# Bulk loads moved to one queue and paced, and the second transform shifted by one group, in a spectral filter fused with a gated FFN

## The chip, the cores and the metric

The kernel runs on one core of a Trainium2 chip. The metric is the device time of one execution in microseconds (us). A profile is one execution, about 2 us shorter than the timed runs of the same kernel, because its span goes from the first to the last instruction.

## The reference, cut to what matters

```python
xn  = layernorm(x)                       # x: 2048 x 640, bf16
s   = irfft2(rfft2(xn) * (A_w_r + 1j * A_w_i))          # filter: 2048 x 321
g   = silu((gelu(xn @ w_gate) * (xn @ w_up)) @ w_down)  # FFN, 1536 wide
out = x + s * g
```

The rows are cut into 16 slabs of 128. The FFN needs the transposed xn and the weights. The filter needs a Fourier transform over all slabs, so it cannot begin before every slab is normalised and folded.

## The kernel before: the parts that matter

TensorE (PE) does nearly all of the work as matmuls. The FFN is a list of 64 items: four groups of twelve gate/up tiles and four downs. All else is hooked behind an item. A scheduler then orders the instructions of each engine, so the order in the source is a priority, not the order on the chip.

Six names of tiles serve as milestones in the profiles: `pg` and `pu` are the gate and up matmuls, `ph` a down, `pa` the fold of a slab, `pzt` the first matmul of the spectral stage (its copy is `ztail`, the name that the prediction uses), and `pv` the first of the inverse.

```python
for q in range(4):                                   # weights: issued by ACT
    nc.scalar.dma_start(out=Wg[:, :, cs], in_=gv[:, :, cs])
    nc.scalar.dma_start(out=Wu[:, :, cs], in_=uv[:, :, cs])
nc.gpsimd.dma_start(out=LANE, in_=tabs["lane"])      # row numbers for the gathers
nc.scalar.dma_start(out=Wd, in_=...)                 # then seven tables, also by ACT
...
def norm(n1):
    if n1 % 3 == 0:   # statistics on DVE
        ...           # bn_stats x2, bn_aggr; POOL adds the epsilon to the variance
    else:             # statistics on ACT, with two accumulating activations
        ...           # POOL turns the sums into mean and variance
    nc.gpsimd.tensor_tensor(out=rstd, in0=rstd, in1=mh, op=ALU.pow)
    nc.vector.tensor_scalar(out=xn, in0=x, scalar1=mean, scalar2=rstd, ...)
    # slabs 0-3: PE transposes and ACT copies; later slabs: a DMA transpose from SP
def fold(n1):
    ...               # DVE: four adds give xf; PE: pa = F1T^T xf; ACT: A = pa
    nc.sync.dma_start(out=D2[:, n1, :], in_=A)       # scratch in HBM
def regroup():        # BU <- D2, needs all sixteen stores
    ...
def gather(G):        # filter weights of group G: four indirect DMAs by POOL
    nc.gpsimd.memset(W[:, :, :, L:LP], 0.0)
    for pm in range(2):
        for ri, wsrc in enumerate((A_w_r, A_w_i)):
            nc.gpsimd.indirect_dma_start(out=W[:, pm, ri, 0:L], in_=wsrc, ...)
def spectral_a(G):    # PE z, ACT Z, PE pe, ACT E, DVE V
def spectral_b(G):    # DVE: M, N = W * V, Y, R;  PE: pi = BD R;  ACT, DVE: IU;  store
...
for i in range(12):
    after[i].append((norm, 4 + i))                   # and the folds
    if i in (5, 7, 9, 11):
        after[i].append((gather, (i - 5) // 2))
after[11].append((regroup,))
for G in range(8):
    i = 14 + 2 * G
    after[i].append((spectral_a, G))
    after[i + 1].append((spectral_b, G))
    if G < 4:
        after[i + 1].append((gather, G + 4))
after[29].append((reload,))
```

So POOL has two jobs: tiny steps (rstd) that every slab waits for, and indirect loads (gathers).

## Time and profile before

The time before is 262.58 us (median of 3 runs, 262.43 to 263.23). In the profile (span 259.9 us):

| milestone | us |
|---|---|
| first gate matmul | 36.36 |
| first down | 68.29 |
| first matmul of the spectral stage | 78.07 |
| first matmul of the inverse | 173.75 |
| end | 259.9 |

The first lines are of the page of the kernel before: busy tenths of PE and of the DMA engines in 40 slices of 6.5 us, and what the DMAs moved.

```profile
PE   0010079999999999999999877779999999999881
DMA  7999993657283032141210110174431012110110
GB/s 216 386 338 327 358 371 83 175 142 196 94 291 115 20 84 63 45 100 44 57 55 0 51 51 3 51 270 186 138 118 53 23 61 70 50 50 3 50 50 25
```

PE is almost idle in the first five slices, busy after them, and dips in slices 23 to 27, which is the end of the spectral stage. The DMA engines are full just where PE is idle.

The timeline of ACT, kernel before: start, duration, engine (ACTq is its DMA issuing), line, operation, and in brackets the idle time before it.

```profile
8.83 4.12 ACTq L208 DMA_DIRECT2D Wu<-in_B_w_up_dram  x1
12.99 2.57 ACTq L207 DMA_DIRECT2D Wg<-in_B_w_gate_dram  x1
...
19.75 4.83 ACTq L212 DMA_DIRECT2D T_77<-tab_t  x1
...
27.39 0.68 ACTq L212 DMA_DIRECT2D IT<-tab_it  x1
28.11 0.69 ACT L245 COPY xnT<-pt 128x640 bf16<-128x640 bf16 x1 [25.37 <-issue]
28.70 0.74 ACT L233 ACTIVATE junk<-X 128x640 bf16<-128x640 bf16 x1
```

An issue normally takes 0.4 to 0.7 us here. Three of them take 2.6 to 4.8 us. ACT does no arithmetic from 2.7 to 28.1 us, because its stream is full of issues, and its first statistics come at 28.70.

What POOL does in that time, timeline of POOL, kernel before:

```profile
7.52 1.01 POOL L282 DMA_INDIRECT W<-in_A_w_r_dram,LANE  x1 [5.33 <-DMA LANE<-tab_lane]
...
27.31 0.95 POOL L282 DMA_INDIRECT W<-in_A_w_i_dram,LANE  x1 [0.30 <-issue]
29.62 0.25 POOL L236 TENSOR_SCALAR mean<-nm 128x1 f32<-128x1 f32 x1 [1.37 <-ACT junk L233]
```

The sixteen gathers of the first four groups run from 7.5 to 28.3 us, about 1.25 us each.

The waits of PE from 0 to 78 us, kernel before (waiter, what it waited for: us in total, times, longest):

```profile
PE pt L244 <- DVE xn L240: 32.6, 3, 17.9
PE pa L260 <- ACT xnT L245: 0.5, 1, 0.5
PE pa L260 <- DVE xf L258: 0.4, 2, 0.2
```

And from 70 to 180 us:

```profile
PE pi L356 <- DVE R L345: 5.8, 7, 1.9
PE pv L375 <- DMA BU<-D_93: 1.4, 1, 1.4
PE pe L317 <- DVE G_1542 L428: 1.2, 1, 1.2
PE ph L423 <- ACT E L324: 0.6, 2, 0.4
```

Once started, PE hardly waits in the fold stage.

### The profile page before, as it was taken

The page shows a single profiled execution, that of the slowest core. Times are in us where ns is not written, and L with a number is a line of the kernel's source. Part 1 is how long each engine was busy: PE and PEld are TensorE (multiplying, and loading weights), DVE is VectorE, ACT ScalarE, POOL GpSimd, SP SyncE. Part 2 cuts the span into 40 slices and gives each one's busy share as a digit, 9 for nine tenths or more (in the row PEclk, how much of TensorE's full clock was granted, in tenths as well). Part 3 has the DMA queues.
Part 4 walks back from the last instruction along what each step waited for, and adds up shares of the span by engine and source line. Part 5 has one row for each costly group of instructions (what it writes and reads, how often), then busy time and mean ns, then how long its engine had stood idle before and what let it go on. Part 6 is the DMA issues. An engine that isn't in the chain of part 4 may idle for free. (4 is left out here: it accounts for less than half of the span.)

```text
span 259.9 us, 3724 instructions
## 1 busy us (share of the span) xinstructions
PE 208.8 (80%) x1348; PEld 118.2 (45%) x1348; DVE 144.5 (56%) x337; ACT 117.5 (45%) x192; POOL 50.2 (19%) x87
## 2 busy tenths in 40 slices
PE   0010079999999999999999877779999999999881
PEld 0000034444575554454454454545567654456660
DVE  1430177998223957756658435448954555653562
ACT  2000689995427264464553514246542445343431
POOL 1777444662000426236000000000000000000000
PEclk9999999999999999999999999999999999999998
DMA  7999993657283032141210110174431012110110
GB/s 216 386 338 327 358 371 83 175 142 196 94 291 115 20 84 63 45 100 44 57 55 0 51 51 3 51 270 186 138 118 53 23 61 70 50 50 3 50 50 25
DMA packets 30385, 31.61 MB, mean 122 GB/s; under 512 B 10384, under 2 KB 28576, under 8 KB 30240
## 3 DMA queue, kind: packets, MB, share of 16 engines
q1 hardware_dynamic: 20992, 20.42, 24.6%
q10 hardware_dynamic: 7808, 8.33, 9.7%
q0 software_dynamic: 1568, 2.64, 4.0%
q8 instruction: 10, 0.16, 0.3%
q14 instruction: 7, 0.06, 0.1%
HBM read 21.53 MB, written 7.88 MB: 113 GB/s over the span
## 5 line engine op out<-in xcount | busy, mean ns | idle before, releaser
L409 PE MATMUL pg<-xnT,Wg 128*128 128x512 bf16 x240 | 63.5, 384 | 0.0
L411 PE MATMUL pu<-xnT,Wu 128*128 128x512 bf16 x240 | 62.2, 380 | 0.0
L423 PE MATMUL ph<-Wd,u 128*128 128x320 bf16 x384 | 53.9, 299 | 1.0 <-ACT E L324 0.6
L423 PEld LDWEIGHTS <-u 128*128 128x128 bf16 x384 | 37.4, 98 | 16.1 <-issue 1.6
L415 DVE TENSOR_TENSOR u<-pu,ge 128x512 bf16<-128x512 f32 x48 | 32.9, 686 | 20.9 <-PE pu L411 17.1
L413 ACT ACTIVATE ge<-pg 128x512 bf16<-128x512 f32 x48 | 28.9, 602 | 18.6 <-PE pg L409 16.1
L411 PEld LDWEIGHTS <-Wu 128*128 128x128 bf16 x240 | 23.2, 98 | 24.5 <-issue 0.8
L409 PEld LDWEIGHTS <-Wg 128*128 128x128 bf16 x240 | 22.3, 99 | 22.7 <-issue 1.1
L426 ACT ACTIVATE th<-ph 128x640 f32<-128x640 f32 x16 | 11.3, 704 | 42.6 <-PE ph L423 42.6
L244 PE MATMUL pt<-ident,xn 128*128 128x128 bf16 x20 | 2.7, 310 | 32.6 <-DVE xn L240 32.6
L282 POOL DMA_INDIRECT W<-in_A_w_r_dram,LANE x16 | 15.4, 965 | 11.0 <-DMA LANE<-tab_lane 5.3
L244 PEld LDWEIGHTS <-xn 128*128 128x128 bf16 x20 | 1.8, 135 | 33.2 <-DVE xn L240 33.2
L282 POOL DMA_INDIRECT W<-in_A_w_i_dram,LANE x16 | 15.4, 965 | 4.8 <-issue 4.8
L356 PE MATMUL pi<-R,BD 128*128 128x322 bf16 x64 | 10.8, 301 | 6.4 <-DVE R L345 5.8
L324 ACT CAST E<-pe 128x644 bf16<-128x644 f32 x16 | 13.1, 888 | 4.6 <-PE pe L322 4.6
L240 DVE TENSOR_SCALAR xn<-X,mean,rstd 128x640 bf16<-128x640 bf16 x10 | 4.4, 443 | 18.4 <-POOL rstd L238 18.2
L359 ACT CAST IU<-pi 128x644 bf16<-128x644 f32 x8 | 5.6, 696 | 19.8 <-PE pi L356 19.8
L245 ACT COPY xnT<-pt 128x640 bf16<-128x640 bf16 x4 | 2.6, 687 | 25.8 <-issue 25.4
L382 ACT CAST Vt<-pv 128x640 bf16<-128x640 f32 x16 | 11.1, 692 | 7.0 <-PE pv L379 7.0
L263 ACT CAST A<-pa 128x640 bf16<-128x640 f32 x16 | 10.9, 697 | 4.3 <-DMA D_92<-A 2.6
L327 DVE TENSOR_TENSOR V<-E 128x644 bf16<-128x644 bf16 x8 | 4.0, 495 | 13.4 <-ACT E L324 13.3
L356 PEld LDWEIGHTS <-BD 128*128 128x128 bf16 x64 | 5.6, 97 | 12.6 <-DVE R L345 9.1
(175 smaller groups left out, 272.4 us busy)
## 6 DMA issues: line engine op xcount, KB each, us to landing
D_93<-IU SPq DMA_DIRECT2D x8, 322.0 KB, 2.9
BU<-D_93 SPq DMA_DIRECT2D x4, 644.0 KB, 6.6
xr<-in_A_x_dram SPq DMA_DIRECT2D x16, 160.0 KB, 2.4
D_92<-A SPq DMA_DIRECT2D x16, 160.0 KB, 2.0
BU<-D_92 SPq DMA_DIRECT2D x4, 640.0 KB, 7.5
out_dram<-res SPq DMA_DIRECT2D x16, 160.0 KB, 1.8
Wg<-in_B_w_gate_dram ACTq DMA_DIRECT2D x4, 480.0 KB, 10.9
Wu<-in_B_w_up_dram ACTq DMA_DIRECT2D x4, 480.0 KB, 10.2
```

The lines of the kernel that those rows point to most:

```text
L263: nc.scalar.copy(out=A, in_=flat(pa)[:, 0:D])
L282: nc.gpsimd.indirect_dma_start(out=W[:, pm, ri, 0:L], out_offset=None, in_=wsrc, in_offset=bass.IndirectOffsetOnAxis(ap=LANE[:, 2 * G + pm ...
L324: nc.scalar.copy(out=E[:, ri].rearrange("p r (i q) -> p r q i", q=2), in_=pe[:, :, 0:LP].rearrange("p r (q i) -> p r q i", q=2))
L356: nc.tensor.matmul(pi[:, pq, 0:LP], lhsT=BD[:, G, ro, ri, :], rhs=R[:, ri, pq, :], start=(ri == 0), stop=(ri == 1))
L359: nc.scalar.copy(out=IU[:, ro], in_=pi[:, :, 0:LP])
L382: nc.scalar.copy(out=flat(Vt), in_=pvf[:, 0:D])
L409: nc.tensor.matmul(pg, lhsT=Wg[:, c, t * P:(t + 1) * P], rhs=xnT[:, c, cols], start=(c == 0), stop=(c == 4))
L411: nc.tensor.matmul(pu, lhsT=Wu[:, c, t * P:(t + 1) * P], rhs=xnT[:, c, cols], start=(c == 0), stop=(c == 4))
L413: nc.scalar.activation(out=ge, in_=pg, func=ACT.Gelu_apprx_tanh)
L415: nc.vector.tensor_tensor(out=u, in0=pu, in1=ge, op=ALU.mult)
L423: nc.tensor.matmul(ph[:, a, 0:320], lhsT=uT[grp, t][:, j * P:(j + 1) * P], rhs=Wd[:, t, 320 * a:320 * a + 320], start=(t == 0), stop=(t == ...
L426: nc.scalar.activation(out=th, in_=ph[:, :, 0:320], func=ACT.Tanh, scale=0.5)
```

## The change

The intent is twofold. The load half puts all bulk loads on SP, in the order in which they are needed, and issues the later ones between the slabs' own transposes and stores; it also moves the statistics of five slabs from ACT to DVE, and the xr loads to POOL. The spectral half emits spectral_b one group later, so that PE has a whole group of other work between E and pi.

```diff
+    ctx.enter_context(tc.manual_schedule(engines={mybir.EngineType.SP}))
-    for q in range(4):
-        nc.scalar.dma_start(out=Wg[:, :, cs], in_=gv[:, :, cs])
-        nc.scalar.dma_start(out=Wu[:, :, cs], in_=uv[:, :, cs])
+    def load_gu(q): ...   # the same two loads, on nc.sync; likewise load_x, load_d, load_tab
+    load_x(0, 1); load_x(1, 2); load_tab("id"); load_x(2, 4); load_gu(0)   # [joined]
+    load_x(4, 8); load_tab("f1"); load_gu(1); load_x(8, 12); load_x(12, 16)
@@ norm
-        if n1 % 3 == 0:
+        if n1 % 3 != 2:
@@ final
-        nc.sync.dma_start(out=xr, in_=xv[:, n1, :])
+        nc.gpsimd.dma_start(out=xr, in_=xv[:, n1, :])
@@ hooks
+    after[0].append((load_gu, 2))
+    after[1].append((load_gu, 3))
+    after[2].append((load_tab, "t2"))
+    after[3].append((load_tab, "fm", "ft"))
+    after[4].append((load_d, 0))
+    after[6].append((load_d, 1))
+    after[8].append((load_tab, "bd", "i1", "im", "it"))
-        after[i + 1].append((spectral_b, G))
+        after[i + 3].append((spectral_b, G))
-            after[i + 1].append((gather, G + 4))
+            after[i + 3].append((gather, G + 4))
-    after[29].append((reload,))
+    after[31].append((reload,))
```

Engines named in `manual_schedule` keep the order of the source; the others are still ordered by the scheduler.

More of the change, by code (lines that the diff above doesn't have):

```diff
@@ L199, with load_x, load_gu, load_d @@
     nc.scalar.activation(out=warm, in_=warm, func=ACT.Gelu_apprx_tanh)
-    for a, b in ((0, 1), (1, 2), (2, 4), (4, 8), (8, 12), (12, 16)):
+    def load_x(a, b):
         nc.sync.dma_start(out=X[:, a:b, :], in_=xv[:, a:b, :])
-        if a == 2:
-            nc.sync.dma_start(out=F1T, in_=tabs["f1"])
-            nc.sync.dma_start(out=ident, in_=tabs["id"])
-    for q in range(4):
+    def load_gu(q):
         cs = slice(q * 384, q * 384 + 384)
-        nc.scalar.dma_start(out=Wg[:, :, cs], in_=gv[:, :, cs])
-        nc.scalar.dma_start(out=Wu[:, :, cs], in_=uv[:, :, cs])
-    nc.gpsimd.dma_start(out=LANE, in_=tabs["lane"])
-    nc.scalar.dma_start(out=Wd, in_=B_w_down.rearrange("(t p) d -> p t d", p=P))
-    for t, k in ((T2, "t2"), (FM, "fm"), (FT, "ft"), (BD, "bd"), (I1T, "i1"), (IM, "im"), (IT, "it")):
-        nc.scalar.dma_start(out=flat(t), in_=tabs[k])
+        nc.sync.dma_start(out=Wg[:, :, cs], in_=gv[:, :, cs])
+        nc.sync.dma_start(out=Wu[:, :, cs], in_=uv[:, :, cs])
+    def load_d(h):
+        nc.sync.dma_start(out=Wd[:, 6 * h:6 * h + 6, :],
+                          in_=B_w_down.rearrange("(t p) d -> p t d", p=P)[:, 6 * h:6 * h + 6, :])
+    def load_tab(*ks):
+        for k in ks:
+            nc.sync.dma_start(out=flat(tiles[k]), in_=tabs[k])
+    tiles = dict(f1=F1T, id=ident, t2=T2, fm=FM, ft=FT, bd=BD, i1=I1T, im=IM, it=IT)
+    nc.gpsimd.dma_start(out=LANE, in_=tabs["lane"])
+    load_x(0, 1)
+    load_x(1, 2)
+    load_tab("id")
+    load_x(2, 4)
+    load_gu(0)
+    load_x(4, 8)
+    load_tab("f1")
+    load_gu(1)
+    load_x(8, 12)
+    load_x(12, 16)
     xn_of, y_of, G_of, W_of = {}, {}, {}, {}
```

## The prediction

> **What bounds it now.** Over the span TensorE (PE) is the bound: busy 80% (208.8 us), nearly 100% from 40 to 140 us and from 180 to 240 (stage table). Its idle time: (a) the start: the first gate matmul runs at 36.4 us; (b) 7.4 us between 140 and 174 us, the end of the spectral stage, waiting for R on DVE (1.9, 1.3, 0.6 us), and 1.4 us for the reload; (c) 7.7 us in the tail from 240.
>
> Why (a): the DMA share is 1.0 (about 350 GB/s) from 10 to 40 us, and ACT issues the weight loads. Its issues block while the queue is full: the timeline has ACT issuing from 0.75 to 28.1 us, one issue lasting 4.8 us, so the statistics of slabs 1 and 2 on ACT start only at 28.7. PE waits 18 us for one xn.
>
> **What changes.**
> 1. All bulk loads go to SP, in order of need, the last between transposes and D2 stores. The Trainium skill, "DMA: Bandwidth & Descriptors", section "Issuing engines are not separate DMA queues", says all issuers share the same 16 engines, so one queue should cost no bandwidth; the trace shows 1.0 share reached. The first matmul needs 1.6 MB, an estimated 5 us at 350 GB/s.
> 2. Statistics of five slabs (1, 4, 7, 10, 13) move from ACT (about 1.95 us a slab) to DVE (0.89+0.20 us).
> 3. xr loads move to POOL; three come first in its order.
> 4. spectral_b one group later: the built PE order has a whole group of filler between e(G+1) and pi(G), and about 8 us of gate/up between the last pi and the first inverse.
>
> **Cost on the critical path.**
> New start: the next limit is POOL, which in order runs LANE, three xr (about 1 us each), then gathers (1.25 us each) between the rstd operations. Estimate: first gather at 6 to 6.6 us, slabs 0-2 normalised at about 14.5, then three more gathers, so rstd of slab 3 at about 21 us, first gate matmul at about 23 us. Gain 13 us.
> Fold stage: DVE was about 90% occupied from 42 to 65 us. It gets seven more slabs of statistics in it (7.6 us), so I sum about 33 us of DVE for 31 us of PE: DVE-bound, 2 to 3 us given back. SP is tight too (issues: about 29 us). The first down (68.3 us before) then starts at about 57.
> Spectral end: of 7.4 us I expect 6 saved.
> Sum: 262.6 - 13 + 2.5 - 6 - about 1 for small waits = 245.
>
> **Predicted: 245 us, 8 in 10 between 238 and 252.** Faster by over 2%: 0.96; within 2%: 0.03; slower: 0.01.
>
> **What would show each step.** ACT's first statistics at about 5 us; xn of slab 3 released by POOL rstd after gathers; first gate matmul at 20 to 26 us; DVE over 90% busy in the fold stage, PE waiting there for xf or u by 2 to 4 us; the first ztail matmul at 66 to 70 us; waits of pi for R under 2 us in total; no wait of pv for the reload; same last 20 us.
>
> **What would make it wrong.** LANE landing early or late shifts the POOL chain by its whole delay. SP in program order: a transpose waiting for xn holds stores and loads behind it; stores hold A buffers, A holds fold matmuls; a late D2 store delays the regroup and PE stalls before ztail. Late weights behind slab traffic. xr on POOL landing late in the tail.

## The result

The changed kernel takes 251.62 us (median of 4 runs, 251.30 to 251.76) against 262.5 us (4 runs). The ratio is 0.9578, with a 95% interval of 0.9558 to 0.9597. All ratios here are the mean time of one kernel's fast runs over the mean of the other's in the same rounds, so they are not quite the ratio of the medians. Executions over 1.5% slower than the fastest of the same kernel are left out of the means. The outputs are right.

The time lies inside the predicted range, close to its upper end, and 6.6 us above the centre. The milestones show that the parts were far less right than the sum:

| us | before | after | difference |
|---|---|---|---|
| first gate matmul | 36.36 | 24.70 | -11.7 |
| first down | 68.29 | 67.54 | -0.8 |
| first spectral matmul | 78.07 | 77.32 | -0.8 |
| first inverse matmul | 173.75 | 157.67 | -16.1 |
| end of the span | 259.9 | 249.8 | -10.1 |

PE starts 11.7 us earlier, and 10.9 us of that are gone 40 us later. The first inverse matmul gains more than the end does, because the shift also moves FFN work from before it to behind it.

The page of the kernel after, the same lines:

```profile
PE   0032947987999999889999999899999999999981
DMA  6996599999967022313101013833111111110110
GB/s 192 348 369 181 115 219 285 249 266 327 220 172 277 0 67 82 111 61 108 53 7 49 14 42 111 364 109 106 52 55 52 52 55 52 52 52 3 52 54 26
```

PE has work in the third slice now, but it has gaps up to the tenth. The DMA engines ease off in slices 4 and 5 and are then full to about 69 us. The dip at the end of the spectral stage is gone.

The timeline of ACT, after: no issues, and the first statistics at 6.12 us instead of 28.70.

```profile
2.04 0.20 ACT L201 ACTIVATE warm<-warm 128x1 f32<-128x1 f32 x1
6.12 0.74 ACT L250 ACTIVATE junk<-X 128x640 bf16<-128x640 bf16 x1 [3.88 <-DMA X<-in_A_x_dram]
```

The timeline of POOL, after: L299 is a gather, L245 and L255 are the steps of rstd.

```profile
22.05 1.65 POOL L255 TENSOR_TENSOR rstd<-rstd,mh 128x1 f32<-128x1 f32 x3
23.84 1.20 POOL L299 DMA_INDIRECT W<-in_A_w_r_dram,LANE  x1
...
33.29 0.95 POOL L299 DMA_INDIRECT W<-in_A_w_i_dram,LANE  x1 [0.30 <-issue]
34.31 0.23 POOL L245 TENSOR_SCALAR rstd<-mva 128x1 f32<-128x1 f32 x1
34.62 0.57 POOL L255 TENSOR_TENSOR rstd<-rstd,mh 128x1 f32<-128x1 f32 x1
```

What hangs on it, timeline of DVE, after:

```profile
22.68 0.98 DVE L257 TENSOR_SCALAR xn<-X,mva,rstd 128x640 bf16<-128x640 bf16 x2 [4.80 <-POOL rstd L255]
...
35.23 0.45 DVE L257 TENSOR_SCALAR xn<-X,mva,rstd 128x640 bf16<-128x640 bf16 x1 [7.59 <-POOL rstd L245]
35.59 0.68 DVE L432 TENSOR_TENSOR u<-pu,ge 128x512 bf16<-128x512 f32 x1
```

And timeline of PE, after:

```profile
24.70 2.29 PE L426 MATMUL pg<-xnT,Wg 128*128 128x512 bf16 x5
26.79 2.34 PE L428 MATMUL pu<-xnT,Wu 128*128 128x512 bf16 x5
...
30.39 1.24 PE L428 MATMUL pu<-xnT,Wu 128*128 128x512 bf16 x5
...
36.32 2.29 PE L428 MATMUL pu<-xnT,Wu 128*128 128x512 bf16 x5 [3.34 <-DVE u L432]
...
67.54 2.74 PE L440 MATMUL ph<-Wd,u 128*128 128x320 bf16 x19
```

These three views are one chain. From 23.84 to 34.24 us POOL issues eight gathers in a row, broken once by a 0.28 us step. The rstd of a slab stands behind them. DVE meets its xn (7.59 us of waiting), and the u that DVE could have computed stands behind that xn in DVE's order; PE needs u to free a buffer in PSUM, the memory that its matmuls write, and waits 3.34 us.

Then PE pays again: five matmuls take 2.29 us at 36.32 but 1.24 us at 30.39. The Trainium skill, "TensorE: Matmul & The Clock Gate", section "Part 1: The HAM clock gate (the "warmup" mystery)", says that after an idle window of about 3.4 us PE runs at half rate until a window of about 3.4 us is busy again. The trace agrees: its record of the granted clock is 0.5 for 3.4 us here, and the mean granted clock from 30 to 40 us is 0.83.

The waits of PE from 0 to 78 us, after:

```profile
PE pt L261 <- DVE xn L257: 21.0, 2, 15.8
PE pu L428 <- DVE u L432: 3.3, 1, 3.3
PE pa L277 <- DVE xf L275: 2.7, 2, 1.4
PE pa L277 <- ACT A L280: 0.8, 1, 0.8
```

The stage from the first gate to the first down takes 42.8 us instead of 31.9. Of these 10.9 us, 6.4 are waits of PE (3.3 + 2.7 + 0.8 - 0.4). About 1.6 are the half-rate matmuls from 36.3 to 40.2 us, counting each at its time at full rate elsewhere in the trace. About 0.9 more is a longer slow phase at the very start: the first five up matmuls take 2.34 us (at 26.79) against 1.47 before (at 38.45), and the first ten gate/up matmuls with one fold take 4.61 us against 3.67. And 1.7 are no loss: the scheduler's new order puts eight more gate/up matmuls (0.216 us each) ahead of the first down. About 0.3 us are not accounted for.

In the spectral stage, waits of PE from 70 to 180 us, after:

```profile
PE pi L373 <- issue: 1.1, 2, 0.7
PE pz L322 <- DVE IU L378: 0.8, 1, 0.8
PE pv L392 <- DMA BU<-D_93: 0.6, 1, 0.6
```

No wait of pi is put down to R any more. With four of 0.2 to 0.4 us that are not shown, the waits sum to 3.6 us instead of 10.0.

### The profile page after: what moved, and what is told of

Same layout as the page of the kernel before. It is cut to its first block, busy times and chain, and to the rows that moved or that the text cites. A ratio compares the mean times of both kernels' runs of the same rounds, so it can differ in the third digit from the quotient of the medians.

```text
span 249.8 us, 3706 instructions
## 1 busy us (share of the span) xinstructions
PE 209.1 (84%) x1327; PEld 119.4 (48%) x1348; DVE 147.8 (59%) x352; ACT 110.5 (44%) x172; POOL 56.3 (23%) x98
## 5 line engine op out<-in xcount | busy, mean ns | idle before, releaser
L426 PE MATMUL pg<-xnT,Wg 128*128 128x512 bf16 x226 | 61.9, 386 | 0.7 <-issue 0.2
L450 POOL DMA_DIRECT2D xr<-in_A_x_dram x16 | 8.8, 551 | 110.9 <-DVE res L454 108.6
L299 POOL DMA_INDIRECT W<-in_A_w_r_dram,LANE x16 | 16.6, 1037 | 6.9 <-issue 3.2
L299 POOL DMA_INDIRECT W<-in_A_w_i_dram,LANE x16 | 15.7, 980 | 4.5 <-issue 4.4
L257 DVE TENSOR_SCALAR xn<-X,mva,rstd 128x640 bf16<-128x640 bf16 x11 | 5.0, 451 | 17.7 <-POOL rstd L255 10.0
L242 DVE BATCH_NORM_STATS2 stats<-X 128x6 f32<-128x320 bf16 x22 | 10.2, 485 | 8.6 <-DMA X<-in_A_x_dram 8.6
L325 ACT CAST Z<-pz 128x1024 bf16<-128x1024 f32 x8 | 8.1, 1011 | 5.2 <-PE pz L322 5.2
```

Source lines behind the costliest of these rows:

```text
L242: nc.vector.bn_stats(out=stats[:, g, :], in_=x[:, 320 * g:320 * g + 320])
L299: nc.gpsimd.indirect_dma_start(out=W[:, pm, ri, 0:L], out_offset=None, in_=wsrc, in_offset=bass.IndirectOffsetOnAxis(ap=LANE[:, 2 * G + pm ...
L426: nc.tensor.matmul(pg, lhsT=Wg[:, c, t * P:(t + 1) * P], rhs=xnT[:, c, cols], start=(c == 0), stop=(c == 4))
```

## The experiments

Twelve kernels ran. The ratios are to the kernel before, run on the same chip. Milestones are from the profiles.

| run | first gate | first down | spectral | inverse | span | ratio, 95% interval |
|---|---|---|---|---|---|---|
| before | 36.36 | 68.29 | 78.07 | 173.75 | 259.9 | 1 |
| after | 24.70 | 67.54 | 77.32 | 157.67 | 249.8 | 0.9578 [0.9558, 0.9597] |
| e1_loads_only | 24.51 | 67.30 | 77.08 | 175.55 | 261.6 | 1.0036 [0.9982, 1.0090] |
| e2_shift_only | 36.05 | 67.98 | 77.76 | 157.02 | 249.2 | 0.9634 [0.9581, 0.9686] |
| e3_pool_program_order | 14.11 | 63.02 | 72.80 | 150.44 | 242.6 | 0.9342 [0.9290, 0.9394] |
| e4_stats_on_act | 21.07 | 62.26 | 72.04 | 149.76 | 241.9 | 0.9323 [0.9260, 0.9386] |
| e5_gathers_last | 14.07 | 52.13 | 72.28 | 152.40 | 244.5 | 0.9308 [0.9254, 0.9361] |
| e6_gathers_last_stats_act | 14.42 | 64.49 | 75.13 | 153.63 | 245.8 | 0.9358 [0.9313, 0.9402] |
| e7_loads_unpaced | 14.11 | 66.21 | 77.87 | 155.42 | 247.6 | 0.9485 [0.9413, 0.9557] |
| e8_shift_gathers_last | 33.41 | 67.53 | 87.67 | 167.06 | 259.2 | 0.9991 [0.9944, 1.0038] |
| e9_old_stats_pool_order | 14.11 | 59.16 | 68.94 | 146.75 | 238.9 | 0.9168 [0.9120, 0.9216] |
| e10_no_early_gathers | 14.08 | 50.37 | 60.15 | 137.84 | 230.0 | 0.8869 [0.8815, 0.8924] |
| e11_late_tables | 20.01 | 58.93 | 68.71 | 147.86 | 240.0 | 0.9262 [0.9200, 0.9323] |
| e12_gathers_after_regroup | 14.14 | 50.56 | 60.34 | 144.09 | 236.2 | 0.9092 [0.9053, 0.9131] |

One caution for reading it. The scheduler puts 120 to 144 gate/up matmuls ahead of the first down, depending on the kernel (120 in before, e2, e8 and e11; 128 in after, e1 and e4; 136 in e3, e5, e6, e9, e10 and e12; 144 in e7), which moves that milestone and the next by up to 5.2 us without any work saved. The ratio is the measure; the milestones say where to look.

### e1: the load half alone

```diff
 (the change, but with these lines as before)
-        after[i + 3].append((spectral_b, G))
+        after[i + 1].append((spectral_b, G))
-    after[31].append((reload,))
+    after[29].append((reload,))
```

> The change without its second half: loads, statistics split and xr on POOL as in the changed kernel, but spectral_b, gather and reload at their old places. Theory A (from the two traces: the load half starts PE 11.7 us earlier but the fold stage gives nearly all of it back, so the first down matmul moves by only 0.75 us, and the gain comes from the spectral half): 260 to 262.5 us, first gate matmul at about 25 us, first down at about 67.5 us, waits of pi for R as before. Rival B (the sum of the prediction: the load half is worth about 10 us): 251 to 254 us.

Measured: 262.76 us, ratio 1.0036. The load half alone gains nothing, although PE starts 11.9 us earlier. At the first down only 1.0 us of it is left, and the waits for R have grown, as the waits of PE from 70 to 180 us of e1 show:

```profile
PE pi L373 <- DVE R L362: 8.3, 6, 5.1
```

### e2: the spectral half alone

```diff
 (the kernel before, with)
-        after[i + 1].append((spectral_b, G))
+        after[i + 3].append((spectral_b, G))
-            after[i + 1].append((gather, G + 4))
+            after[i + 3].append((gather, G + 4))
-    after[29].append((reload,))
+    after[31].append((reload,))
```

> The kernel before with only the spectral half (spectral_b and gather one group later, reload two items later); loads on two queues as before. Theory A: 252 to 254 us, that is 9 to 10 us of gain from this half alone, first gate matmul at 36.4 and first down at about 68.3 us as before, waits of pi for R near zero. Rival B (prediction): 256 to 257 us (6 us).

Measured: 252.07 us, ratio 0.9634, or 9.6 us of 262.5. So this half carries nearly the whole gain of the change. All waits of pi for R are gone, and the waits of PE from 70 to 180 us sum to 2.2 us. The product of the ratios of the two halves is 0.967; the change itself is at 0.958. The halves together may be 1% better than that product, about as much as the intervals allow, and I make nothing of it.

What remains to be explained is why 11.7 us of earlier start are worth nothing.

### e3: POOL in the order of the source

The scheduler had put gathers ahead of rstd steps. Here POOL keeps the order of the source, where the first gather comes behind item 5.

```diff
-    ctx.enter_context(tc.manual_schedule(engines={mybir.EngineType.SP}))
+    ctx.enter_context(tc.manual_schedule(engines={mybir.EngineType.SP, mybir.EngineType.Pool}))
```

> The changed kernel with the instructions of POOL, too, kept in program order: the gathers of A_w_r and A_w_i and the xr loads then stand behind the rstd operations of slabs 0 to 9, instead of 16 gathers standing among those of slabs 0 to 6. Theory P (the gathers on POOL hold back rstd, that holds back xn of slabs 3 and 6, and through DVE's order also u and PE): first gate matmul at 14 to 17 us, no wait of DVE for rstd over 2 us in the fold stage, 240 to 245 us. Rival D (DVE is overloaded by the statistics moved to it): earlier start, but DVE over 90% busy and first down not before 62 us, 246 to 249 us. Rival S (the order on SP holds D2 stores and with them A and PE): 248 to 252 us.

Measured: 244.52 us, ratio 0.9342, 2.4% better than the change. The first gate moves to 14.1 us. The gathers are still in the way later on: each batch of four stands between rstd steps. DVE waits 13.0 us for rstd from 14 to 66 us, and PE 9.0 us for xf. So theory P had the time right, but not its "no wait of DVE for rstd over 2 us": the longest is 4.0 us.

### e4: the old split of the statistics

```diff
-        if n1 % 3 != 2:
+        if n1 % 3 == 0:
```

> The changed kernel with the old split of the statistics (DVE for slabs 0, 3, 6, 9, 12, 15; ACT for the others). Theory P: the fold stage is not set by DVE's load, so 250 to 253 us, within 1% of the changed kernel. Rival D: 5.5 us less DVE work in the fold stage, so 3 to 5 us faster, 247 to 249 us.

Measured: 243.80 us, ratio 0.9323. I had put the weight on POOL and expected little of this run; that was a miss, and even rival D's 247 to 249 us was too slow. Moving five slabs of statistics to DVE costs about 2.7% (0.9578 against 0.9323). It was meant to relieve ACT, but once ACT issues no loads it has time: in the change ACT is busy only 3.2 to 5.4 us of every 10 from 0 to 60, while DVE is at 9.5 and 9.3 of 10 from 40 to 60.

### e5 and e6: gathers behind the norms

e5 is e3 with the first sixteen gathers moved behind the last norm; e6 is e5 with the old statistics.

```diff
-        if i in (5, 7, 9, 11):
-            after[i].append((gather, (i - 5) // 2))
     after[11].append((regroup,))
+    for G in range(4):
+        after[12].append((gather, G))
```

> The changed kernel with POOL in program order and the 16 gathers of the first four frequency groups emitted after the last rstd (about 20 us of POOL work, not needed before the first spectral_b). Statistics as in the changed kernel (11 slabs on DVE). Theory P (gathers on POOL between the rstd operations starve DVE and then PE; e3 showed the same stalls moved later): first gate matmul at 14 us, no wait of DVE for rstd over 2 us, first down at 49 to 53 us, 231 to 236 us. Rival D (DVE's load sets the fold stage): first down at 54 to 58 us, 236 to 240 us. Rival S (the order of SP sets it): no better than e3, 242 to 245 us.

> The run with the gathers last, with the old split of the statistics as well (DVE 6 slabs, ACT 10). Theory P alone: the same as the run before within 1.5 us. Theory P with D: another 2 to 4 us faster, 229 to 234 us. If ACT becomes the limit (20 us of statistics in the fold stage): slower than the run with the statistics on DVE.

Measured: 245.48 us for e5 (median of three fast runs; the slow fourth took 249.00; ratio 0.9308) and 246.57 us for e6 (0.9358). Both miss what I expected, e5 by 10 us, and with the gathers here the old split of the statistics brings nothing: the two intervals overlap. The rstd chain is free, and yet the time is no better than in e3. POOL now issues the gathers back to back at the end of the fold stage (38.0 to 58.4 us in e6), and there the other engines stop for long stretches. These are lines of the waits from 40 to 66 us, e6:

```profile
ACT ge L430 <- remote: 9.9, 1, 9.9
DVE u L432 <- ACT ge L430: 7.0, 1, 7.0
DVE xf L274 <- issue: 6.9, 1, 6.9
ACT A L280 <- issue: 5.7, 2, 5.4
PE pa L277 <- ACT A L280: 4.4, 1, 4.4
```

"issue" and "remote" mean that the profile shows no releaser. Around 50.6 us ACT and DVE both go on within 0.1 us of each other, after waiting on PE's semaphore, though by its records PE had done that work at 47 us. The granted clock stays at 0.5 for 17 us.

### e7: all loads up front

```diff
 (e6, with these right behind load_x(12, 16) instead of in items 0 to 8)
+    load_gu(2)
+    load_gu(3)
+    load_d(0)
+    load_d(1)
+    load_tab("t2", "fm", "ft", "bd", "i1", "im", "it")
```

> As the run with the gathers last and the old split of statistics, but all bulk loads issued at the start on SP in the same order of need, not paced between transposes and D2 stores. If the pacing matters: transposes and D2 stores wait behind about 9 MB of loads (an estimated 27 us at 350 GB/s), fold matmuls stop for A, 6 us or more slower than the paced one. If it does not: within 2 us.

Measured: 249.66 us, ratio 0.9485 against 0.9358 of e6. So giving up the pacing costs e6 about 3 us, between the two readings (6 or more, within 2). It is not a clean price of the pacing: e7 has a stall like e6's, beside gathers that run from 43.2 to 63.9 us (DVE waits 11.6 us for a u, with no visible releaser, and PE 9.8 us for an A, the copy of a fold), and what the loads add to it was not separated.

### e8: gathers last with the old loads

```diff
 (e2, with)
+    ctx.enter_context(tc.manual_schedule(engines={mybir.EngineType.Pool}))
 (and the gathers moved as in e5)
```

> The kernel before with the spectral half of the change (as e2) and with POOL in program order and the gathers after the last rstd. Theory P says that in the kernel before the gathers ran in the shadow of ACT's blocked load issues (7.5 to 28 us) and cost nothing: 251 to 253 us, as e2. If the gathers cost time there too: 245 to 249 us.

Measured: 262.34 us, ratio 0.9991, where I had expected e2's 252; neither expectation fits. With the old loads, moving the sixteen gathers out of the idle start costs all that the shift gains. They then run from 56 to 77 us, and the same long stalls as in e6 appear (DVE once 9.3 us). So the idle start is by far the cheaper place. The run does not show that the gathers are free there. The timeline of PE, e8:

```profile
33.41 2.29 PE L411 MATMUL pg<-xnT,Wg 128*128 128x512 bf16 x5
```

In e2 that first gate runs at 36.05. Without gathers in the start ACT's issues end sooner (first statistics at 25.63 us, 28.40 in e2), so at their old place the gathers cost up to 2.6 us of the start. That their transfers slow the loads down is the likely reason; it was not tested.

### e9: both repairs that helped alone

e3 and e4 together.

> The changed kernel with both repairs that helped alone: the old split of the statistics and POOL in program order. Theory F (before the regroup the DMA engines have 62 to 69 us of work in every kernel so far, so ztail cannot start before about 71 us, whatever the start): first gate near 14, ztail 71 to 73, time 241 to 244, no better than either repair alone. Theory S (the repairs remove separate waits of POOL and DVE and add): ztail 65 to 68, time 235 to 239.

Measured: 240.30 us, ratio 0.9168. The two repairs add, though not fully: the separate gains over the change are 2.4 and 2.6 points of the ratio, and together they give 4.1. The time falls between the ranges of theory F (241 to 244) and theory S (235 to 239), and so does the start of the spectral stage at 68.9 us (F: 71 to 73, S: 65 to 68). Neither theory as written is right.

### e10: no early gathers (wrong result)

```diff
 (e6, with)
     def gather(G):
+        if G < 4:
+            nc.gpsimd.memset(W, 0.0)
+            W_of[G] = W
+            return
```

> The kernel with gathers last and the old statistics, without the 16 gathers of groups 0 to 3 (their weights are zero: wrong on purpose). They move 1.3 MB of about 19.4 MB that land before ztail. Theory G (gathers running beside dense work cause the long stalls of ACT, DVE and PE at 49 to 66 us): no wait over 4 us in 40 to 66 us, first down near 56, ztail 60 to 65, time 230 to 236. Theory F (the DMA work before the regroup is the floor): ztail about 4 to 5 us earlier than the 75.1 us with gathers, so 70 to 71, time 240 to 242.

Measured: 231.91 us, ratio 0.8869; the result is wrong (relative error 0.028). Against e6 this is 4.9 points of the ratio, about 13 us. The long stalls are gone, the granted clock is 0.999, and PE is 94% busy from 10 to 60 us (46.9 us of 50). So the sixteen gathers, at the place where e6 has them, cause the stalls. That is theory G's time. As theory F was written, from the bytes, it is refuted: 1.3 MB less should have been worth 4 to 5 us ahead of the spectral stage, and 15 us came.

### e11: tables after the regroup

```diff
 (e4, with)
-    after[8].append((load_tab, "bd", "i1", "im", "it"))
     after[11].append((regroup,))
+    after[12].append((load_tab, "bd", "i1", "im", "it"))
```

> The changed kernel with the old statistics split, and the 1.4 MB of tables that only the filter and the inverse need loaded after the regroup instead of in item 8. Theory F: about 4 us less DMA work before the regroup, so ztail about 68 instead of 72, time 239 to 241. Rival (ztail waits for the compute engines, not for DMA): ztail 71 to 73, time 243 to 245.

Measured: 242.19 us, ratio 0.9262 against 0.9323 of e4, with intervals that overlap. The spectral stage starts 3.3 us earlier, as F said, but eight gate/up matmuls fewer stand ahead of it (1.7 us), so only 1.6 us are real, and the span is 1.9 us shorter. The time lies between the two expectations. Taking 1.4 MB out of the crowded stage is worth something like 2 us, half of what theory F gave for a pure DMA limit; as the intervals overlap, no gain at all is not excluded.

### e12: gathers held back until the regroup

POOL first copies one column of the regrouped slabs into a tile that nobody needs. As POOL keeps the order of the source, the gathers stand behind that copy.

```diff
 (e6, with)
+    def hold_pool():
+        nc.gpsimd.tensor_copy(out=warm, in_=hop["B"][:, 12, 0:1])
 ...
+    after[12].append((hold_pool,))
     for G in range(4):
         after[12].append((gather, G))
```

> The kernel with gathers last and the old statistics (246.6 us), with one tiny POOL copy from the regrouped slabs ahead of the 16 gathers, so that they start only when the DMA work of the fold stage is over (about 60 us) and run back to back to about 80 us, with 8 instead of 20 us or more of other DMA traffic beside them. Theory C (the gathers hurt where they meet the full DMA queues of the fold stage): ztail near 60 as without the early gathers, no wait over 4 us in 60 to 80 us, granted clock above 0.98, time 231 to 235, the best version. Theory B (16 gathers back to back stall the other engines wherever they run): ztail near 60, but stalls of 5 us or more and half clock between 60 and 80 us, time 238 to 247.

Measured: 237.94 us (6 runs, 237.01 to 239.62), ratio 0.9092: correct, and the fastest correct version, 9% below before and 5% below the change. One tiny instruction on POOL is worth 7 us against e6, by the ratios. The timeline of PE, e12:

```profile
14.14 2.29 PE L429 MATMUL pg<-xnT,Wg 128*128 128x512 bf16 x5 [0.71 <-ACT xnT L262]
...
50.56 9.94 PE L443 MATMUL ph<-Wd,u 128*128 128x320 bf16 x72
...
60.34 0.39 PE L316 MATMUL pzt<-T,BU 128*128 128x128 bf16 x4
```

Up to here it equals the kernel without early gathers. The stalls without a visible releaser do not come back, although the gathers run back to back from 66 to 87 us; that speaks against theory B's mechanism. But the run also misses the 231 to 235 us of theory C, and some of what B foretold is there: PE waits 4.5 us once, ACT 5.4 us once, the granted clock is 0.5 for 3.4 us from 76.7 us, and the time is at the lower edge of B's range. These waits have a reason that is plain in the trace. The hold waited for the last quarter of the regroup and let the gathers start at 65.2 us, not 60. Timeline of POOL, e12:

```profile
65.16 0.18 POOL L295 CAST warm<-BU 128x1 f32<-128x1 bf16 x1 [27.60 <-DMA BU<-D]
```

The first filter product then had to wait for its gathers, and the G of a down stood behind it on DVE, which PE needed. Timeline of DVE and of PE, e12:

```profile
72.79 0.83 DVE L359 TENSOR_TENSOR M<-W,V 128x1288 bf16<-128x1288 bf16 x1 [4.26 <-DMA W<-in_A_w_i_dram,LANE]
```

```profile
75.95 0.44 PE L337 MATMUL pe<-FT,ztail 128*128 128x322 bf16 x2 [4.53 <-DVE G L448]
```

In e10 that M starts at 68.18. The gathers of group 0 leave POOL at 70.91 and release M at 72.79. The Trainium skill, "Perfetto Trace Analysis", section "DMA Instruction — SWDGE (GPSIMD)", says that the recorded end of such an instruction is the end of descriptor generation, not of the data movement; the 1.9 us between the two times agree with that. A hold on the first quarter, or only three groups held back, may take these 4.5 us away; that was not run.

## Why the prediction was right or wrong, point by point

The sum missed by 7.4 us in the profile, nearly all of it in one term. That the time still fell inside the range, by 0.4 us, was luck. Each term against the profile:

| term | predicted, us | measured, us |
|---|---|---|
| first gate matmul | -13 | -11.7 |
| given back up to the first down | +2.5 | +10.9 |
| spectral stage and small waits, up to the end | -7 | -9.4 |
| sum | -17.5 | -10.1 |

The scheduler's reordering moved 1.7 us of work from the third row to the second. Without it they would read +9.2 and -7.7.

**The start: right in mechanism and nearly in size.** ACT's first statistics come at 6.12 us (predicted about 5), xn of slab 3 waits 4.80 us for rstd behind gathers, and the first gate runs at 24.70 (predicted 20 to 26, about 23).

**The fold stage: the step that failed.** The prediction said "DVE-bound, 2 to 3 us given back. SP is tight too", and "The first down (68.3 us before) then starts at about 57." It started at 67.54, and 10.9 us were given back, of which 1.7 are only reordered work. The first ztail matmul came at 77.32 instead of 66 to 70, and PE waited 6.0 us for xf and u instead of 2 to 4. DVE was indeed over 90% busy, but only from 40 to 60 us (9.52 and 9.33 of 10). From 20 to 40 us DVE was at 4.89 and 3.75 of 10, and PE at 6.67 and 6.61. That stretch was limited by POOL. The prediction saw gathers in front of the rstd of slab 3 and charged them to the start; it did not go on to the eight gathers that follow from 23.8 us and stand in front of the next slabs. Before the change they were nearly free, since POOL had no statistics from ACT up to 28 us. The load half removed the idle time and so uncovered them. e3, which only puts POOL in the order of the source, gains 2.4% of the time before; e8 shows the price of a bad place from the other side; and e10 and e12 show how much room there was: with the gathers out of the fold stage the first down comes at about 50.5 us.

**The statistics: right sign, too small.** The prediction counted the statistics moved to DVE as part of the 2 to 3 us given back. e4 measures the new split alone at 2.7% of the time, about 7 us at the end; 3.6 us of it already show at the first gate. e3 and e4 share some of this loss, since e9 shows that they do not add fully, and with the gathers last (e5, e6) the split makes no measurable difference.

**The DMA engines: missing from the sum.** The prediction called only "late weights behind slab traffic" a risk. The DMA share from 40 to 60 us rose from about 0.55 to 1.05, as loads that used to be over by then now meet transposes and stores. e7 (3 us for giving up the pacing, beside stalls) and e11 (about 2 us for 1.4 MB, with overlapping intervals) suggest that this traffic costs something. But e10 and e12 keep a share of 1.0 from 10 to 60 us with PE 94% busy, so a full share alone is not proof of a limit.

**The spectral stage: right in mechanism, 1 to 3 us too small.** "I expect 6 saved" of 7.4 us. The prediction counted the idle time of PE from 140 to 174 us only. The waits of PE over the whole stage sum to 10.0 us, and e2, the shift alone, leaves 2.2 of them and gains 9.6 us; in the change itself, less the reordered work, the last term is -7.7 against -7. The waits of pi for R are gone (under 2 us were predicted); pv still waits 0.6 us for the reload, where none was predicted. The last 20 us are the same, as predicted (7.5 us idle of PE in the last 19.8 us after, 7.6 in the last 19.9 before).

**What stays open.** The stalls of 5 to 12 us in e5 to e8 have no visible releaser. e10 shows that the gathers cause them in e6, and e12 that gathers back to back do not do so everywhere. I had suspected the full DMA queues; but in e8 the DMA share was 0.60 and 0.25 where it stalled. Late instruction loads do not fit either: e6 has packets of the page's instruction queues at 44.4 us and next at 64.4 us, and its stalls end at 50.6 and 61.3. Besides its later start, e12 differs in that no D2 stores or transposes of SP run beside its gathers; that rival was not tested. I cannot say which resource it is.

## What to carry to other kernels

When a change removes an idle stretch, list what was running for free in its shadow, on every engine, and ask where that work lands and what stands behind it in the same instruction stream; here sixteen indirect loads on POOL, together with the new split of the statistics, ate most of an earlier start of 11.7 us (e9, which repairs both, gets 4.1% of the time before back). Long asynchronous work must not share an in-order engine with tiny steps that a whole pipeline waits for: keep that engine in the order of need, and hold the long work back with a real dependence until the crowded stage is over (with the old split of the statistics, this took the changed kernel from 252 to 238 us). And sum the waits of the bound engine over the whole stage, not only where the dip is visible.

## What the Trainium skill lacked or had wrong

- "DMA: Bandwidth & Descriptors", section "Issuing engines are not separate DMA queues", says that issuing on several engines saves only the sequencer's time to start the DMAs, which is usually small. That section lacks the reverse: here ACT, issuing while the DMA share was 1.0, could not compute meanwhile. Single issues of ACT took 2.6 to 4.8 us, and ACT had its first statistics at 28.7 us instead of 6.1 us. That the start was then worth nothing in e1 (ratio 1.0036) was for other reasons.
- No page says how long POOL is taken up by indirect loads issued in a row: here mostly 0.95 us each at a pitch of 1.25 us, so sixteen of them keep POOL from other work for 20 us.
- "SBUF — State Buffer", section "SBUF: two separate sides", names the port pair shared by DVE and GpSimd as the only contention among engines. The runs with gathers at the end of the fold stage show stalls of 5 to 10 us on ACT as well as on DVE (ACT ge 9.9 us, DVE xf 6.9 us in e6), and none without a releaser in e12 with the same gathers later. In e6 the stalled ACT and DVE both wait on PE's semaphore, so this is no proof of another contention; that section does not explain the stalls, and the cause is open.
